# Score slots and down-projection parts as four 32x32 matmuls instead of one 32x128

## The chip, the cores and the metric

The kernel runs on one core of a Trainium2 chip. The metric is the device time of one execution in microseconds (us), the median over several runs. The core has five engines that work side by side and meet only at semaphores: TensorE (matmuls; its weight loads have a row of their own in the profile, PEld), VectorE (DVE), ScalarE (ACT), GpSimd (POOL) and SyncE (SP), which starts transfers. Matmul results land in PSUM, which has eight banks of 128 partitions x 512 float32; all other tiles (names ending in `_sb`) are in SBUF, 128 partitions wide.

TensorE's array has 128 rows (the contracted dimension) and 128 columns (the result's partitions). A matmul with a `tile_position` uses a part of the array whose sizes are multiples of 32, and matmuls on separate parts can run at once. Three shapes occur in the kernel: full (128 rows x 128 columns), column tiles (128 x 32, four side by side) and row tiles (32 x 128, four one under another). The profile writes them 128*128, 128*32 and 32*128.

## The reference

The input `x` is 2048 x 512. With `xn` the layer norm of `x`, the output is `x + s * g`:

- `s` is attention with 32 heads of 16 dimensions for the queries and a single shared head for keys and values: `q = xn @ wq`, `k = xn @ wk`, `v = xn @ wv`, softmax of `q k^T / 4` over 2048 keys, times `v`, and then `@ wo`.
- `g = silu(silu(xn @ w1) @ w2)`, where `w1` is 512 x 1792 and `w2` 1792 x 512.

All inputs are bfloat16. Because the contraction of a score is only 16 long (one head), a full-height matmul would leave most of the array's rows unused.

## The kernel before

**Tiling of the attention.** Queries are cut into four chunks of 512 and heads into four octets, which gives 16 tiles of q (`mk_q`, 128 partitions = eight heads x 16 dimensions, 512 queries). Two heads share a strip of 32 partitions, so each tile is handled as two groups `g` (32 groups in all), and in a group strip `i` (0 to 3) belongs to one head. `kt_sb` holds the transposed keys, repeated in each strip for the even and, shifted by 16 partitions with zeros, for the odd heads. One *score slot* is one strip `i` and one block `kt` of 128 keys: a matmul with 32 contracted rows (`kt_sb` 32 x 128 as the weights, `qt_sb` 32 x 512 as the moving operand) that fills a whole PSUM bank, 128 keys x 512 queries. There are 32 x 4 x 16 = 2,048 slots. `s_mm` issues one.

**Phases.** `do_S` puts three or four slots, with different strips and different banks, into one *score phase*. They sit in separate row groups of the array and run at once. Only the last matmul of a phase increments TensorE's semaphore. Banks 0 to 6 are shared by slots and jobs; bank 7 takes the attention's output.

**What follows a slot.** Most slots go to ScalarE (`act_step`, L1717), which takes the exponential of one to three banks at a time and writes `pa_sb`. The others go to VectorE (`pass_d`, L1002), which forms an approximate exponential with integer arithmetic (`db_sb`); GpSimd adds three shifted versions to it (`split`, L1202, `ds_sb`). `do_pv` (L1282) then multiplies all of these with the values: four column tiles at once, each 128 keys x 32 columns, into bank 7. `make_norm` divides by the sums.

**Jobs.** The other products (queries, `h` = the up projection, `z` = the down projection, `w` = the output projection) are jobs made by `product`. A job holds one bank and has rounds; a round is four column tiles (`col4`, L511), one contracted block of 128. If a phase has only three slots, a job can put one strip of 32 contracted rows of its last block into the idle row group: that is `piece` (L618), a 32-row matmul that adds into the job's bank. Four pieces make up one round. 76 matmuls are of this kind.

**What sets the order.** `Planner` and the steps below it (`pe_step`, `act_step`, `generic_step`) simulate the engines with fixed durations and write the order of every engine out before the program is built: `MM` = 216 ns for a matmul of 512 columns however many run at once, `SWITCH` = 105 ns between two modes of the array (`S` row tiles, `C` column tiles, `F` full), `T_P` and so on for the others. `finalize` turns the dependencies into semaphore waits, and each engine runs its list in order. `do_S` places a phase as one operation of 216 ns (two slots on the same strip would count double).

Of the kernel before, what the change touches and what calls it, by code (L numbers as in the profile page):

```python
# [15 lines left out]
P = 128  # L16
DH = 16
NQ = 512
LN_EPS = 1e-5
T_ISSUE, T_SWDGE = 450.0, 1000.0  # L20
J_BASE, J_END, MIXJ = 0.1, 1.0, 2
# [274 lines left out]
def bass_recurrent_scan__grouped_kv_mqa__dense_activation_silu__prompt_kernel(  # L296
# [14 lines left out]
    F = B_w1.shape[1]  # L311
    NT, NC, NDC, NFT = S // P, S // NQ, D // P, F // P
    NH = D // DH
# [5 lines left out]
    QSCALE = float(DH) ** -0.5  # L319
    assert D == 512 and S % NQ == 0 and F % P == 0  # L320

# [3 lines left out]
    NQR, NON = 4, 2 * NOC  # L325

    with ExitStack() as es:
        def sb(name, shape, dt):
            return es.enter_context(nc.sbuf_tensor(name, shape, dt))
# [10 lines left out]
        kt_sb = sb("kt_sb", [P, 2, S], BF16)  # L340
        v_sb = sb("v_sb", [P, K + 1, NKT, 48], BF16)
        qt_sb = sb("qt_sb", [P, NQR, NQ], BF16)
        pa_sb = sb("pa_sb", [P, NPA * NQ], BF16)
        db_sb = sb("db_sb", [P, NDB, 4 * NQ], U16)
        ds_sb = sb("ds_sb", [P, NDS, 4 * NQ], U16)
        f_sb = sb("f_sb", [P, 2, NQ], FP32)
# [31 lines left out]
        def bank(b):  # L378
            return ps[:, b * 512:(b + 1) * 512]
# [87 lines left out]
        for n in first:  # L467
            b = a + n
            tiles = range(a, b)
            g = a // 4  # L470
            y, w, h = rstd_sb[:, a:b], var_sb[:, 0, a:b], var_sb[:, 1, a:b]

            def dv(fn, reads, writes, pre):
                return pl.add(Task(DV, 66.0, fn, reads, writes, g, [pre] if pre is not None else []))
            t = pl.add(Task(DV, 66.0, lambda v, a=a, b=b, w=w: v.tensor_scalar(
                w, mv_sb[:, a:b, 1], LN_EPS, None, op0=ALU.add), [("mv", i) for i in tiles], [("ve", a)], g,
                [aggr[i] for i in tiles]))
# [31 lines left out]
        def col4(h, b, lhs, rhs, start, stop, n=NQ):  # L509
            for j in range(4):  # L510
                last = h.matmul(bank(b)[32 * j:32 * (j + 1), 0:n], lhsT=lhs(j), rhs=rhs, start=start, stop=stop,  # L511
                                tile_position=(0, 32 * j), skip_group_check=True)
            return last
# [93 lines left out]
        def product(jb, lhs, rhs, needs):  # L607
            n = len(jb.rounds)

            def rnd(k):  # L610
                def mk(b):
                    last = jb.left == 1
                    return lambda pe: col4(pe, b, lambda j: lhs(k, slice(0, P), 32 * j, 32), rhs(k, slice(0, P)), k == 0, last)
                return mk

            def piece(k, i, last):
                rows, b = slice(32 * i, 32 * i + 32), jb.bank
                return (lambda pe: pe.matmul(bank(b), lhsT=lhs(k, rows, 0, P), rhs=rhs(k, rows), start=False, stop=last,  # L618
                                             tile_position=(32 * i, 0), skip_group_check=True), needs(k))
            jb.rounds = [(rnd(k), needs(k), MM) for k in range(n)]  # L620
            jb.piece = piece

# [240 lines left out]
            return k  # L863

        def s_mm(pe, b, g, i, kt):
            return pe.matmul(bank(b), lhsT=kt_sb[32 * i:32 * i + 32, g % 2, kt * P:(kt + 1) * P],  # L866
                             rhs=qt_sb[32 * i:32 * i + 32, (g // 2) % NQR, :],
                             start=True, stop=True, tile_position=(32 * i, 0))

        def v_lhs(j, g, kt):  # L870
            return v_sb[:, j, kt, DH:48] if g % 2 == 0 else v_sb[:, j, kt, 0:32]
# [134 lines left out]
        def do_S(t):  # L1006
# [87 lines left out]
            def emit(pe, mm=tuple(mm)):  # L1094
                h = None
                for (b, g, i, kt) in mm:
                    h = s_mm(pe, b, g, i, kt)
                if extra is not None:
                    h = extra(pe)
                return h  # L1100
# [22 lines left out]
            while late and len(seen) < 4 and len(dslots) < (2 if bl < two else 1) and want_d():  # L1123
                used = set(seen)
                d = pick_d(used, t)
                if d is None:
                    break
                b = late.pop(0)
                _, g, i, kt = d
                seen[i] = 1  # L1130
                t1 = max(op.t0 + 10.0, pl.ready(PE, s_reads(g, i, kt), [("ps", b)]))
                pool_free.remove(b)
                pl.place(PE, MM, lambda pe, b=b, g=g, i=i, kt=kt: s_mm(pe, b, g, i, kt), s_reads(g, i, kt), [("ps", b)], t0=t1)
                pl.set_mode("S")
                pass_d(b, *d)
                dslots.append(d)
                st["late"] = st.get("late", 0) + 1
# [682 lines left out]
```

## Time and profile before

| | |
|---|---|
| median of 3 runs | 669.84 us (669.71 to 669.84) |
| span of the profiled execution, first to last instruction | 667.9 us |
| its own time | not listed apart; the span lies 1.94 us below the median |
| mean granted TensorE clock | 1.000 |
| matmuls / weight loads | 8,972 / 8,973 |
| score slots (L866) | 2,048, mean record 384 ns |
| parts of the down projection (L618) | 76, mean record 384 ns |
| exponentials on ScalarE (L1717) | 670, 617.0 us of records |
| VectorE on slots (L1002) | 736, 475.4 us of records |
| GpSimd shifts (L1202) | 544, 554.0 us of records |

How to read it: a record of a matmul lasts from its start to the modelled arrival of its last result, so records of matmuls that stream one after another overlap, and busy time is the union of the records. A group is written `line engine operation out<-in`, then the tile of the array as rows*columns, the operand, the count, and after the bar the busy time and the mean ns of one. In a timeline a line is a start in us, a length in us (from the first start to the last end where a count stands behind), and the operation. In a list of waits a line is who waited, for whom, the total in us, how often, and the longest.

### The profile page before, as it was taken

Reading aid. Unit: us, or ns where it says so; the run is one execution under the profiler, and the core shown is the slowest. Engines: PE = TensorE matmul, PEld = TensorE weight load, DVE = VectorE, ACT = ScalarE, POOL = GpSimd, SP = SyncE. Lnnn points to the kernel's source line nnn. Section 1 sums busy time; section 2 is a strip of 40 time slices with the busy share of each in tenths; the row PEclk is TensorE's granted clock in tenths of the full one; section 3 lists DMA queues with packets and bytes.
Section 4 is the critical chain, followed back from the end, with each engine's and each line's share of the span. In section 5 each row is a group of like instructions: output and inputs, shape, how many; then the busy total and the mean of one; then the engine's idle time right before and its main releaser. Section 6 shows DMA issues by size and latency. Waiting matters only on the chain.

```text
span 667.9 us, 21230 instructions
## 1 busy us (share of the span) xinstructions
PE 657.8 (98%) x8972; PEld 190.3 (28%) x8973; DVE 613.6 (92%) x1093; ACT 652.8 (98%) x767; POOL 561.9 (84%) x560
## 2 busy tenths in 40 slices
PE   8999999999999999999999999999999999999997
PEld 4322222222222222222222222222222322222222
DVE  8989999999899999989999899999999999998995
ACT  6999999999999999999999999999999999999997
POOL 3059889999898889998989888999899989897972
PEclk9999999999999999999999999999999999999999
DMA  9500000000000000000000010000000000000000
GB/s 302 164 9 2 3 1 2 2 3 2 1 2 18 19 18 18 1 2 2 2 2 2 18 32 18 2 2 2 2 2 2 2 18 18 17 18 2 2 2 33
DMA packets 11501, 12.86 MB, mean 19 GB/s; under 512 B 1808, under 2 KB 10768, under 8 KB 11408
## 3 DMA queue, kind: packets, MB, share of 16 engines
q1 hardware_dynamic: 10928, 10.78, 5.0%
q8 instruction: 72, 1.18, 0.7%
q0 software_dynamic: 192, 0.46, 0.2%
q10 hardware_dynamic: 288, 0.26, 0.1%
q14 instruction: 21, 0.17, 0.1%
HBM read 8.95 MB, written 2.10 MB: 17 GB/s over the span
## 4 chain that ended last, share of the span: by engine, by line
PE 88%; ACT 6%; DVE 4%; issue 1%; DMA 0%; ACTq 0%; DVEq 0%
PE ps L1282 38%; PE ps L866 29%; PE ps L511 20%; ACT pa_sb L1717 6%; DVE db_sb L1002 1%; DVE stats_sb L458 1%; ACT t_sb L669 1%; DMA ds_sb<-in_A_x_dram 0%; DVE fin_sb L719 0%; PE ps L527 0%; DVE xnT_sb L538 0%; DVE xn_sb L487 0%; DVE ob_sb L731 0%; DVE mv_sb L462 0%; DVE on_sb L1316 0%
## 5 line engine op out<-in xcount | busy, mean ns | idle before, releaser
L1717 ACT ACTIVATE pa_sb<-ps 128x1024 bf16<-128x1024 f32 (+2 forms) x670 | 617.0, 1027 | 4.8 <-PE ps L866 3.5
L1202 POOL INT64_ADD ds_sb<-db_sb x544 | 554.0, 1040 | 64.2 <-DVE otr_sb L1342 31.7
L1002 DVE TENSOR_SCALAR db_sb<-ps 128x512 uint16<-128x512 f32 x736 | 475.4, 683 | 40.0 <-PE ps L866 28.6
L1282 PE MATMUL ps<-ds_sb,v_sb 128*32 128x512 bf16 x2208 | 268.7, 383 | 0.0
L866 PE MATMUL ps<-qt_sb,kt_sb 32*128 32x512 bf16 x2048 | 251.2, 384 | 3.9 <-ACT pa_sb L1717 0.9
L1282 PE MATMUL ps<-pa_sb,v_sb 128*32 128x512 bf16 x1316 | 240.9, 382 | 0.0
L1282 PE MATMUL ps<-db_sb,v_sb 128*32 128x512 bf16 x736 | 169.3, 383 | 0.0
L866 PEld LDWEIGHTS ps<-qt_sb,kt_sb 32*128 32x128 bf16 x2048 | 62.8, 91 | 276.7 <-ACT pa_sb L1717 151.2
L1282 PEld LDWEIGHTS ps<-ds_sb,v_sb 128*32 128x32 bf16 x2208 | 65.6, 95 | 62.3 <-issue 44.6
L511 PE MATMUL ps<-xnT_sb,w_sb 128*32 128x512 bf16 x896 | 71.7, 383 | 0.0
L1282 PEld LDWEIGHTS ps<-pa_sb,v_sb 128*32 128x32 bf16 x1316 | 58.8, 95 | 37.9 <-issue 24.7
L511 PE MATMUL ps<-w_sb,u_sb 128*32 128x512 bf16 x820 | 64.1, 383 | 0.0
L1282 PEld LDWEIGHTS ps<-db_sb,v_sb 128*32 128x32 bf16 x736 | 42.2, 95 | 20.2 <-issue 14.7
L669 ACT ACTIVATE t_sb<-ps 128x512 bf16<-128x512 f32 x72 | 44.9, 623 | 0.0
L671 DVE SCALAR_TENSOR_TENSOR u_sb<-t_sb,ps 128x512 bf16<-128x512 bf16 x56 | 38.2, 683 | 1.0
L618 PE MATMUL ps<-w_sb,u_sb 32*128 32x512 bf16 x76 | 29.2, 384 | 0.0
L511 PEld LDWEIGHTS ps<-xnT_sb,w_sb 128*32 128x32 bf16 x896 | 17.1, 94 | 26.1 <-issue 21.1
L1359 POOL DMA_DIRECT2D kt_sb<-kt_sb x4 | 2.3, 566 | 23.9 <-DVE var_sb L481 8.1
L1338 DVE STREAM_TRANSPOSE f_sb<-ps 128x512 f32<-128x512 f32 x31 | 21.9, 706 | 0.0
L511 PEld LDWEIGHTS ps<-w_sb,u_sb 128*32 128x32 bf16 x820 | 15.2, 95 | 22.5 <-issue 19.3
L511 PE MATMUL ps<-wo_sb,on_sb 128*32 128x512 bf16 x256 | 18.9, 383 | 0.0
L511 PE MATMUL ps<-xnT_sb,wq_sb 128*32 128x512 bf16 x240 | 18.7, 384 | 0.1
(74 smaller groups left out, 180.8 us busy)
## 6 DMA issues: line engine op xcount, KB each, us to landing
w_sb<-in_B_w_dram SPq DMA_DIRECT2D x2, 1792.0 KB, 13.4
xr_sb<-in_A_x_dram SPq DMA_DIRECT2D x16, 128.0 KB, 2.6
out_dram<-ob_sb SPq DMA_DIRECT2D x16, 128.0 KB, 1.7
ds_sb<-in_A_x_dram SPq DMA_DIRECT2D x3, 512.0 KB, 6.6
wq_sb<-in_A_wq_dram SPq DMA_DIRECT2D x1, 512.0 KB, 4.9
wo_sb<-in_A_wo_dram SPq DMA_DIRECT2D x1, 512.0 KB, 16.2
kt_sb<-kt_sb POOLq DMA_DIRECT2D x4, 112.0 KB, 3.7
ds_sb<-in_A_x_dram ACTq DMA_DIRECT2D x2, 128.0 KB, 2.9
```

The source lines that it names most:

```text
L458: ts_ = pl.add(Task(DV, 593.0, lambda v, t=t: v.bn_stats(stats_sb[:, t, :], x_tile(t)), [xkey(t)], [("st", t)], 1 + j, gate=(lambda j=j: S ...
L511: last = h.matmul(bank(b)[32 * j:32 * (j + 1), 0:n], lhsT=lhs(j), rhs=rhs, start=start, stop=stop, tile_position=(0, 32 * j), skip_group_c ...
L618: return (lambda pe: pe.matmul(bank(b), lhsT=lhs(k, rows, 0, P), rhs=rhs(k, rows), start=False, stop=last, tile_position=(32 * i, 0), skip ...
L669: t1 = Task(AC, 490.0, lambda a: a.activation(t_sb[:, k, :], src, ACT.Tanh, scale=scale), [held], [("t", k)], 0, [t0])
L671: t2 = Task(DV, T_P, lambda v: v.scalar_tensor_tensor(out=dst, in0=t_sb[:, k, :], scalar=1.0, in1=src, op0=ALU.add, op1=ALU.mult), [held, ...
L866: return pe.matmul(bank(b), lhsT=kt_sb[32 * i:32 * i + 32, g % 2, kt * P:(kt + 1) * P], rhs=qt_sb[32 * i:32 * i + 32, (g // 2) % NQR, :], ...
L1002: bt.P[i] = pl.add(Task(DV, T_P, lambda v: v.tensor_scalar(db_sb[:, bt.b, i * NQ:(i + 1) * NQ], bank(b), 128.0 * LOG2E, 128.0 * (SHIFT_BET ...
L1202: whole["po"].append(pl.add(Task(PO, T_P64, lambda g, cols=cols: g.int64_add(ds_sb[:, s, cols].bitcast(U64), db_sb[:, bt.b, cols].bitcast( ...
L1282: h = pe.matmul(bank(OB)[32 * i:32 * (i + 1), cols], lhsT=lhs, rhs=rhs, start=s0, stop=s1, tile_position=(0, 32 * i), skip_group_check=True)
L1338: t1 = pl.add(Task(DV, T_TR, lambda v: v.transpose(f_sb[:, k, :], bank(OB)), [("ps", OB)], [("F", k)], 1, [norm.get(("m", g - 2))]))
L1359: kt1[c] = pl.add(Task(PO, T_SWDGE, lambda e: e.dma_start(kt_sb[DH:P, 1, cols], kt_sb[0:P - DH, 0, cols]), [("kt0", k) for k in range(4 * ...
L1717: op = pl.place(AC, 0.8333 * NQ * n + T_AF, lambda a: a.activation(pa_sb[:, s * NQ:(s + n) * NQ].rearrange("p (b n) -> p b n", n=NQ), ps3[ ...
```

## The change

A constant `SW = 32` is added. `s_mm` and `piece` each issued one matmul of 32 rows x 128 columns. Now each issues four, for columns 0 to 31, 32 to 63, 64 to 95 and 96 to 127 of the weights, at tile positions `(32 * i, c)`, into the partitions `c` to `c + 31` of the same bank. Moving operand, bank, accumulation flags and results are the same. The last of the four is what is returned, and so it carries the increment if the slot is the last of its phase. Nothing in the planner is changed, so the order and the waits of all engines are the same list as before.

```diff
+SW = 32
...
             def piece(k, i, last):
                 rows, b = slice(32 * i, 32 * i + 32), jb.bank
-                return (lambda pe: pe.matmul(bank(b), lhsT=lhs(k, rows, 0, P), rhs=rhs(k, rows), start=False, stop=last,
-                                             tile_position=(32 * i, 0), skip_group_check=True), needs(k))
+                def emit(pe):
+                    for c in range(0, P, SW):
+                        h = pe.matmul(bank(b)[c:c + SW, :], lhsT=lhs(k, rows, c, SW), rhs=rhs(k, rows), start=False, stop=last,
+                                      tile_position=(32 * i, c), skip_group_check=True)
+                    return h
+                return emit, needs(k)
...
         def s_mm(pe, b, g, i, kt):
-            return pe.matmul(bank(b), lhsT=kt_sb[32 * i:32 * i + 32, g % 2, kt * P:(kt + 1) * P],
-                             rhs=qt_sb[32 * i:32 * i + 32, (g // 2) % NQR, :],
-                             start=True, stop=True, tile_position=(32 * i, 0))
+            for c in range(0, P, SW):
+                h = pe.matmul(bank(b)[c:c + SW, :], lhsT=kt_sb[32 * i:32 * i + 32, g % 2, kt * P + c:kt * P + c + SW],
+                              rhs=qt_sb[32 * i:32 * i + 32, (g // 2) % NQR, :],
+                              start=True, stop=True, tile_position=(32 * i, c), skip_group_check=True)
+            return h
```

## The prediction

> **What bounds the kernel now.** I read the page first (busy shares, chain, groups), then the busy time of the steady stretch, then the waits, then TensorE's timeline at full resolution.
>
> The page, busy shares and the chain that ended last:
> ```profile
> PE 657.8 (98%) x8972; PEld 190.3 (28%) x8973; DVE 613.6 (92%) x1093; ACT 652.8 (98%) x767; POOL 561.9 (84%) x560
> ...
> PE 88%; ACT 6%; DVE 4%; issue 1%; DMA 0%; ACTq 0%; DVEq 0%
> PE ps L1282 38%; PE ps L866 29%; PE ps L511 20%; ACT pa_sb L1717 6%; DVE db_sb L1002 1%; DVE stats_sb L458 1%; ACT t_sb L669 1%; DMA ds_sb<-in_A_x_dram 0%; DVE fin_sb L719 0%; PE ps L527 0%; DVE xnT_sb L538 0%; DVE xn_sb L487 0%; DVE ob_sb L731 0%; DVE mv_sb L462 0%; DVE on_sb L1316 0%
> ...
> L866 PE MATMUL ps<-qt_sb,kt_sb 32*128 32x512 bf16 x2048 | 251.2, 384 | 3.9 <-ACT pa_sb L1717 0.9
> ...
> L618 PE MATMUL ps<-w_sb,u_sb 32*128 32x512 bf16 x76 | 29.2, 384 | 0.0
> ```
> TensorE and ScalarE are both busy 98%, but the chain is 88% TensorE. The two changed operations are L866 (2,048 score slots) and L618 (76 parts): 2,124 matmuls out of 8,972, and L866 alone is 29% of the chain. By its names (`w_sb,u_sb`) L618 is the down projection alone.
>
> The waits of the weight loads, the only place where TensorE waits for another engine (time, times, longest):
> ```profile
> PEld ps L866 <- ACT pa_sb L1717: 151.2, 355, 0.7
> PEld ps L866 <- DVE db_sb L1002: 106.6, 240, 0.7
> ...
> PEld ps L866 <- DVE qt_sb L628: 5.4, 12, 0.5
> ...
> PEld ps L866 <- DVE fin_sb L719: 4.4, 10, 0.5
> ```
> This is 267.6 us in 617 waits and looks like semaphores, but is not. The timeline of three microseconds shows what it is:
> ```profile
> 299.88 0.39 PE L866 MATMUL ps<-qt_sb,kt_sb 32*128 32x512 bf16 x3
> 300.20 0.39 PE L1282 MATMUL ps<-ds_sb,v_sb 128*32 128x512 bf16 x2
> 300.21 0.39 PE L1282 MATMUL ps<-pa_sb,v_sb 128*32 128x512 bf16 x2
> 300.43 0.61 PE L511 MATMUL ps<-xnT_sb,wq_sb 128*32 128x512 bf16 x8
> 300.97 0.39 PE L866 MATMUL ps<-qt_sb,kt_sb 32*128 32x512 bf16 x3
> 301.29 0.62 PE L511 MATMUL ps<-xnT_sb,wq_sb 128*32 128x512 bf16 x8
> 301.84 0.39 PE L866 MATMUL ps<-qt_sb,kt_sb 32*128 32x512 bf16 x3
> 302.16 0.40 PE L1282 MATMUL ps<-ds_sb,v_sb 128*32 128x512 bf16 x4
> ```
> Rows of column tiles (128*32) follow each other every 0.216 us. Between a phase of row tiles (32*128) and a run of column tiles, in either direction, the next start comes some 0.31 us after the last: about 97 ns of emptying the array. In that case the weight loads sit idle for 0.42 us whatever the semaphores do. 617 x 0.42 = 259 us, so real waiting for ScalarE and VectorE is only 267.6 - 259 = 8.5 us, and by the start stamps it lies in 92 phases (92 ns each). TensorE sets the pace.
>
> **The stamps in ns.** The trace has every start in ns; the timeline rounds to 10. Counted over the whole trace there are 641 phases of row tiles, 440 with three matmuls and 201 with four (440 x 3 + 201 x 4 = 2,124). What I use:
> - spacing of a load-matmul pair inside a phase: 3.35 ns. The same for the four pairs that open a run of column tiles: 3.33 ns;
> - first load to first matmul: 4.5 ns in a row-tile phase, 1.5 ns in a column-tile run;
> - last matmul's start to the first matmul of the next mode: 314.5 ns from row to column tiles, 311.5 ns from column to row tiles, 317 ns from row tiles to full 128*128 matmuls, 309 ns from full ones to column tiles, all with 512 columns;
> - a column run of a single round, its weights not loaded ahead: 322 ns to the next mode (19.02 us; also a run of three at 44.91 us).
>
> **The change, part by part.** Instructions: 3 x 2,124 = 6,372 more matmuls and as many weight loads; matmuls go from 8,972 to 15,344. Order, waits and semaphores do not change: one increment on a phase's last matmul, as now; the planner's costs are untouched. So the sum is over phases: time from a phase's first load to the next mode's first matmul.
>
> Before, three slots: 4.5 + 2 x 3.35 + 314.5 = 325.7 ns; four: 4.5 + 3 x 3.35 + 314.5 = 329.1 ns.
>
> After, three slots are 12 pairs of 32 columns, loaded like column tiles: 1.5 + 11 x 3.35 + 322 = 360.4 ns; four are 16 pairs: 1.5 + 15 x 3.35 + 322 = 373.8 ns. The 512 columns still stream at once in all tiles.
>
> Difference: 34.7 ns x 440 + 44.7 ns x 201 = 15.3 + 9.0 = 24.3 us. The parts (L618) are slots in these phases and so are in it.
>
> Unknown prices, with ends:
> - *Spacing of 12 to 16 pairs.* No stretch has more than four tiles at once. Low end: all parts start together, which makes every phase 1.5 + 322 = 323.5 ns, 2.2 to 5.6 ns shorter than now, -2 us in all. High end: 25 ns a matmul, the start-to-start of the 16-column matmuls of the value projection (L583), 9 x 25 to 12 x 25 ns a phase, some 159 us. I take 3.35: both kinds of phase with separate tiles and 512 columns show it, while L583's matmuls all use the same array.
> - *End of the phase.* 322 (loads not ahead, 32 columns) or 314.5 (128 columns). At 314.5 the sum is 24.3 - 641 x 7.5 ns = 19.5 us. I take 322, since the parts are of 32 columns.
> - *The emptying itself.* Ends: gone, or as now. Row tiles to full matmuls changes only the row size, full to column tiles only the column size, and each keeps its 95 to 103 ns. I take it as it is, for the new switch (32*32 to 128*32) is of the first kind.
> - *Waits that soak it up.* Of the 8.5 us none or all may go. A stalled phase waits 92 ns and each phase brings 35 ns, 38%: I take 3.2 us off.
>
> Nothing else covers the 24.3 us: in the steady stretch TensorE is busy throughout.
> ```profile
> 40.00:655.00 615.00, 613.47 (x8319) 171.03 (x8315) 571.79 (x954) 611.07 (x699) 552.98 (x544) 1.00 0.03 7
> ```
> Columns are the stretch, then TensorE, loads, VectorE, ScalarE, GpSimd, clock and DMA. ScalarE's 611 holds overlap of successive records (1,024-element exponentials can start 904 to 921 ns apart and last 1,048); by those least intervals it has 17.8 us to spare. It and VectorE get more slack. A slot's result comes 27 to 40 ns later to them, which counts only in the few waits above. Instruction supply: a three-slot phase with two rounds has 24 + 16 instructions in 0.9 us, 22 ns each; the zero-filled rounds (256 columns) ran 24 rounds of eight in 109 ns, 13.7 ns each, so I cost it at nothing. If that cover is gone it costs some ns a pair.
>
> Sum: +24.3 - 3.2 = +21.1 us. The profiled span is 667.9; the median of the three runs, 669.84, is 1.94 above it, the launch around the span, which I keep. 667.9 + 21.1 = 689.0, plus 1.94: 690.9 us, +3.1%.
>
> Two rules of the Trainium skill bear here. "TensorEngine Tiling (Array Packing)", Gotcha 2: Feature Incompatibilities, says that column tiling excludes Fast Weight Load; the trace agrees as far as 322 against 314.5 ns go, and with the rule the sum is 24.3 us, without it 19.5. "TensorE: Matmul & The Clock Gate", The mechanism, says that weight loads overlap with running matmuls only where the row group differs; that is the last rival below.
>
> **Rivals.** (1) *The emptying goes or shrinks, as 32*32 and 128*32 tiles have the same width.* For it: every switch in the trace has a 128-wide side, so this one is not shown. Against: the switches above cost the same whichever size changes. 641 x 2 x 97 ns = 124 us would leave TensorE; ScalarE then bounds, and its 17.8 us are the most that goes: 652 us, with a fixed order 656. It decides from 21.1 us / 1,282 = 16 ns off each switch. Chance 0.08.
> (2) *Loads of one column strip for different row groups get in each other's way*, 25 ns apart as in L583, rather than 13.4 (4 x 3.35): the last load comes (n-1) x 25 + 10 ns after the first, 60 and 85 ns rather than 37 and 50; 440 x 23 + 201 x 35 = 17 us more, 708 us. Against: the present loads of 128 columns cover every strip and follow at 3.35 ns. Chance 0.09, with any shortfall of instructions in it.
> (3) *Hidden*, since ScalarE paces: within 0.2%. The 8.5 us of waits against 613 us busy speak against it. Chance 0.03.
> (4) *A load waits for the matmul before it in the same row group.* The four parts of a slot would stream one after another: 6,372 x 216 ns = 1,376 us more, 2,046 us. Against: four column tiles share all rows, and their loads start 3.3 ns apart under running matmuls, so by that rule the trace disagrees. Chance 0.02.
> The forecast has 0.78.
>
> **How the numbers follow.** The forecast's own ends: 19.5 - 8.5 = +11 (681) to 24.3 with nothing soaked up (694), somewhat more if the spacing is 4 to 5 ns (700). The range goes from 682 to rival (2)'s 708; outside lie rivals (1), (3), (4) and a little of the rest, under 0.2. About 0.2% is what a measurement of this kernel tells from no change. Faster: rival (1) and a rest, 0.09; same: rival (3), 0.03; slower 0.88.
>
> **What would show it.** Right: 15,344 matmuls; the L866 group's busy time grows by about 641 x 37 ns, from 251 to some 273 us; a three-slot phase starts its 12 matmuls within 37 ns, and the next mode follows 322 ns after the last; VectorE's and ScalarE's busy time stays and their shares fall by 3%. Wrong: the next mode less than 300 ns after a phase's last matmul (rival 1); starts in a phase spread over 60 ns or more, or in steps after every fourth (rival 2); 216 ns between parts of one slot (rival 4); TensorE idle grown while the phase did not (3).

## The result, and the profile after

The changed kernel takes 692.59 us (median of 3 runs, 692.33 to 693.86) against 669.84 us. The ratio is 1.0346, 95% interval 1.0327 to 1.0365: slower by 22.8 us. The profiled execution has a span of 690.5 us and a time of 692.33. The forecast was 690.9 us within 682 to 708.

The page of the changed kernel: busy shares, instruction queue, chain, and the groups of the slots, their weight loads and the parts (the line numbers have moved by up to 7; L872 was L866, L621 was L618, L1289 was L1282):
```profile
span 690.5 us, 33975 instructions
...
PE 678.0 (98%) x15345; PEld 210.0 (30%) x15345; DVE 623.3 (90%) x1093; ACT 665.2 (96%) x767; POOL 561.0 (81%) x560
...
q8 instruction: 122, 2.00, 1.2%
...
PE 90%; DVE 5%; ACT 3%; issue 1%; DMA 0%; ACTq 0%
...
L872 PE MATMUL ps<-qt_sb,kt_sb 32*32 32x512 bf16 x8192 | 272.1, 385 | 5.2 <-ACT pa_sb L1724 0.9
...
L872 PEld LDWEIGHTS ps<-qt_sb,kt_sb 32*32 32x32 bf16 x8192 | 81.8, 87 | 279.3 <-ACT pa_sb L1724 151.6
...
L621 PE MATMUL ps<-w_sb,u_sb 32*32 32x512 bf16 x304 | 30.0, 385 | 0.0
```
TensorE has 6,373 more matmul records (6,372 matmuls; the profile before lacks the record of one) and is busy 20 us longer; L872 alone grew from 251.2 to 272.1 us. ScalarE's and VectorE's shares fell by 2 points each, although their busy times grew, from 652.8 to 665.2 us and from 613.6 to 623.3 us. The chain is TensorE's at 90%.

TensorE's timeline in three phases:
```profile
310.39 0.42 PE L872 MATMUL ps<-qt_sb,kt_sb 32*32 32x512 bf16 x12
310.74 0.39 PE L1289 MATMUL ps<-ds_sb,v_sb 128*32 128x512 bf16 x2
310.75 0.39 PE L1289 MATMUL ps<-pa_sb,v_sb 128*32 128x512 bf16 x2
310.96 0.60 PE L512 MATMUL ps<-xnT_sb,wq_sb 128*32 128x512 bf16 x8
311.50 0.42 PE L872 MATMUL ps<-qt_sb,kt_sb 32*32 32x512 bf16 x12
311.85 0.61 PE L512 MATMUL ps<-xnT_sb,wq_sb 128*32 128x512 bf16 x8
312.39 0.42 PE L872 MATMUL ps<-qt_sb,kt_sb 32*32 32x512 bf16 x12
```
The twelve matmuls of a three-slot phase still run at once, but a phase's records now cover 0.42 us instead of 0.39, and the next mode starts 0.35 us after the phase's first matmul instead of 0.32. By the stamps in ns, over all 641 phases (medians):

| | before | after |
|---|---|---|
| first to last matmul, three slots (440 phases) | 7 ns | 37 ns |
| first to last matmul, four slots (201 phases) | 10 ns | 50 ns |
| last matmul of a phase to the column tiles | 314.5 ns | 314.5 ns |
| last column tile to the phase's first matmul | 312 ns | 309 ns |
| first matmul to the phase's signal, three slots | 415 ns | 490 ns |
| first matmul to the phase's signal, four slots | 424 ns | 524 ns |
| waiting at phase starts (last matmul to the phase's first load, beyond 308 ns), in all | 8.2 us | 10.3 us |

The span's growth of 22.6 us is then accounted for in three items. The phases: 440 x 30 + 201 x 40 ns = 21.2 us, less 641 x 3 ns = 1.9 us because the first matmul follows its load sooner: 19.3 us. The waits: 2.1 us. And a single pause in the first stage, 1.05 us beyond the usual spacing, which the forecast did not have:
```profile
14.55 0.28 PE L512 MATMUL ps<-zer_sb 128*32 128x256 bf16 x4
15.46 1.29 DVE L459 BATCH_NORM_STATS2 stats_sb<-ds_sb 128x6 f32<-128x512 bf16 x2
15.72 0.10 PEld L512 LDWEIGHTS ps<-zer_sb 128*32 128x32 bf16 x4 [1.27 <-issue]
15.72 0.29 PE L512 MATMUL ps<-zer_sb 128*32 128x256 bf16 x4 [0.89 <-issue]
```
These are filler rounds on zeros; from the start of the last before the gap to the first after it 1.16 us pass, with no semaphore to wait for ("issue"). The sum, 22.45 us, is within 0.2 us of the 22.6 us.

### The profile page after: what moved, and what is told of

Its sections match the earlier page's. It is cut to its first block, busy times and chain, and to the rows that moved or that the text cites. A ratio compares the mean times of both kernels' runs of the same rounds, so it can differ in the third digit from the quotient of the medians.

```text
span 690.5 us, 33975 instructions
## 1 busy us (share of the span) xinstructions
PE 678.0 (98%) x15345; PEld 210.0 (30%) x15345; DVE 623.3 (90%) x1093; ACT 665.2 (96%) x767; POOL 561.0 (81%) x560
## 4 chain that ended last, share of the span: by engine, by line
PE 90%; DVE 5%; ACT 3%; issue 1%; DMA 0%; ACTq 0%
PE ps L1289 36%; PE ps L872 33%; PE ps L512 20%; DVE db_sb L1009 3%; ACT pa_sb L1724 3%; DVE u_sb L676 0%; DMA ds_sb<-in_A_x_dram 0%; PE ps L554 0%; PE ps L528 0%; DVE fin_sb L724 0%; PE ps L621 0%; PE ps L650 0%; DVE on_sb L1323 0%; DVE stats_sb L459 0%; ACTq L328 0%
## 5 line engine op out<-in xcount | busy, mean ns | idle before, releaser
L1724 ACT ACTIVATE pa_sb<-ps 128x1024 bf16<-128x1024 f32 (+2 forms) x670 | 628.3, 1011 | 15.1 <-PE ps L872 9.0
L1009 DVE TENSOR_SCALAR db_sb<-ps 128x512 uint16<-128x512 f32 x736 | 482.6, 685 | 53.7 <-PE ps L872 36.7
L872 PE MATMUL ps<-qt_sb,kt_sb 32*32 32x512 bf16 x8192 | 272.1, 385 | 5.2 <-ACT pa_sb L1724 0.9
L1289 PE MATMUL ps<-ds_sb,v_sb 128*32 128x512 bf16 x2208 | 268.7, 383 | 0.0
L1289 PE MATMUL ps<-pa_sb,v_sb 128*32 128x512 bf16 x1316 | 240.7, 382 | 0.0
L1289 PE MATMUL ps<-db_sb,v_sb 128*32 128x512 bf16 x736 | 169.3, 383 | 0.0
L872 PEld LDWEIGHTS ps<-qt_sb,kt_sb 32*32 32x32 bf16 x8192 | 81.8, 87 | 279.3 <-ACT pa_sb L1724 151.6
L1289 PEld LDWEIGHTS ps<-ds_sb,v_sb 128*32 128x32 bf16 x2208 | 65.6, 95 | 62.4 <-issue 45.9
L1289 PEld LDWEIGHTS ps<-pa_sb,v_sb 128*32 128x32 bf16 x1316 | 58.8, 95 | 37.8 <-issue 26.3
L1289 PEld LDWEIGHTS ps<-db_sb,v_sb 128*32 128x32 bf16 x736 | 42.2, 95 | 20.3 <-issue 15.2
L621 PE MATMUL ps<-w_sb,u_sb 32*32 32x512 bf16 x304 | 30.0, 385 | 0.0
L512 PEld LDWEIGHTS ps<-xnT_sb,w_sb 128*32 128x32 bf16 x896 | 17.2, 94 | 25.8 <-issue 21.1
L512 PEld LDWEIGHTS ps<-w_sb,u_sb 128*32 128x32 bf16 x820 | 15.2, 95 | 22.6 <-issue 19.3
```

Source lines behind the costliest of these rows:

```text
L621: h = pe.matmul(bank(b)[c:c + SW, :], lhsT=lhs(k, rows, c, SW), rhs=rhs(k, rows), start=False, stop=last, tile_position=(32 * i, c), skip_ ...
L872: h = pe.matmul(bank(b)[c:c + SW, :], lhsT=kt_sb[32 * i:32 * i + 32, g % 2, kt * P + c:kt * P + c + SW], rhs=qt_sb[32 * i:32 * i + 32, (g ...
L1009: bt.P[i] = pl.add(Task(DV, T_P, lambda v: v.tensor_scalar(db_sb[:, bt.b, i * NQ:(i + 1) * NQ], bank(b), 128.0 * LOG2E, 128.0 * (SHIFT_BET ...
L1289: h = pe.matmul(bank(OB)[32 * i:32 * (i + 1), cols], lhsT=lhs, rhs=rhs, start=s0, stop=s1, tile_position=(0, 32 * i), skip_group_check=True)
L1724: op = pl.place(AC, 0.8333 * NQ * n + T_AF, lambda a: a.activation(pa_sb[:, s * NQ:(s + n) * NQ].rearrange("p (b n) -> p b n", n=NQ), ps3[ ...
```

## The experiments

The theory after the result: what a phase pays is the spread of the starts of its matmuls, 3.35 ns for each; the emptying between two tile shapes is as before; the signal comes later still, and the waits hang on it; the pause is a lack of instructions. Each run was made beside the kernel before, whose median was 669.69 to 669.79 us.

### Two matmuls of 32x64

```diff
-SW = 32
+SW = 64
```


> Two matmuls of 32x64 a slot instead of four of 32x32, so 6 or 8 a phase instead of 12 or 16. Theory (each further load-matmul pair costs 3.35 ns of TensorE at the phase's end and some 5 ns of its signal): 440 x 10 + 201 x 13.4 ns = 7.1 us of phase, less up to 1.9 if the first matmul follows its load sooner, plus under 1 us of waits: 676 to 678 us; the last matmul of a phase starts 17 or 24 ns after the first, the signal comes some 425 or 435 ns after the last matmul. Rival (narrow tiles as such cost, by a fixed amount a phase): near 692 us if any column split costs it, near 670 if only 32 columns do.

Measured: 683.60 us, ratio 1.0207 (1.0191 to 1.0222). Both ideas missed: it is 6 us above the theory and 8 or 14 us off either form of the rival. The spread is as the theory had it: 17 and 23 ns from first to last matmul. But the next mode comes 328 ns after the last matmul instead of 314.5, and the signal 438 and 447 ns after it, 12 to 13 ns over the 425 and 435 expected. The groups of weight loads give a hint (columns: busy us and mean ns of one behind the bar); first of the kernel before, then of this one:
```profile
L866 PEld LDWEIGHTS ps<-qt_sb,kt_sb 32*128 32x128 bf16 x2048 | 62.8, 91 | 276.7 <-ACT pa_sb L1717 151.2
```
```profile
L872 PEld LDWEIGHTS ps<-qt_sb,kt_sb 32*64 32x64 bf16 x4096 | 76.4, 101 | 276.9 <-ACT pa_sb L1724 149.5
```
A load of 64 columns takes 101 ns, of 128 columns 91, of 32 columns (above) 87. The later end of the phases makes 13.5 ns x 641 = 8.7 us, and the spread 440 x 10 + 201 x 13 ns = 7.0 us, less 1.9 us as after the change and less 0.3 us of waits (7.9 us against 8.2): 13.5 us, against a measured growth of 13.8. So the cost has two parts, the number of matmuls and a later end of the phase; with 32 columns the second is nil. That the second comes from the length of the phase's last load is argued and not shown: against 32 columns the load grows by as much as the phase's end (14 ns), but against 128 columns by 10 ns only, and no run changes the load alone.

That 128 columns load faster than 64 agrees with the Trainium skill, "TensorEngine Tiling (Array Packing)", Gotcha 2: Feature Incompatibilities, by which narrow tiles do without Fast Weight Load. "TensorE: Matmul & The Clock Gate", LDWEIGHTS (loading the stationary operand), has the time as columns / 1.2 ns, which by estimate is 27 ns for 32 columns more; here the loads of 64 columns are 14 ns longer than those of 32, so the measurement decides for half of it.

### The same matmuls strip by strip

```diff
...
-                for (b, g, i, kt) in mm:
-                    h = s_mm(pe, b, g, i, kt)
-                if extra is not None:
-                    h = extra(pe)
+                for c in range(0, P, SW):
+                    for (b, g, i, kt) in mm:
+                        h = s_mm(pe, b, g, i, kt, [c])
+                    if extra is not None:
+                        h = extra(pe, [c])
```
(Not shown: `s_mm` and `piece` take the list of column starts in place of their own range.)


> The same 12 or 16 matmuls of a phase, issued column strip by column strip (strip 0 of every slot, then strip 1) instead of slot by slot. Theory (only the count matters): 692.6 us within 1 us, spacing 3.35 ns. Rival (loads of one column strip for different row groups hinder each other): spacing over 3.35 ns, 5 us or more slower; rival (loads in one row group hinder each other, partly): faster by as much.

Measured: 692.64 us, ratio 1.0341 (1.0326 to 1.0357). Spread 37 and 50 ns, next mode 314.5 ns later, waits 10.3 us: the same in every number. Neither loads of one strip nor loads in one row group hinder each other at 3.35 ns apart. The forecast's rivals (2) and (4) fall.

### Slots split and parts whole; parts split and slots whole

The first undoes the `piece` half of the change:
```diff
-                def emit(pe):
-                    for c in range(0, P, SW):
-                        h = pe.matmul(bank(b)[c:c + SW, :], lhsT=lhs(k, rows, c, SW), rhs=rhs(k, rows), start=False, stop=last,
-                                      tile_position=(32 * i, c), skip_group_check=True)
-                    return h
-                return emit, needs(k)
+                return (lambda pe: pe.matmul(bank(b), lhsT=lhs(k, rows, 0, P), rhs=rhs(k, rows), start=False, stop=last,
+                                             tile_position=(32 * i, 0), skip_group_check=True), needs(k))
```
The second undoes the `s_mm` half:
```diff
-            for c in range(0, P, SW):
-                h = pe.matmul(bank(b)[c:c + SW, :], lhsT=kt_sb[32 * i:32 * i + 32, g % 2, kt * P + c:kt * P + c + SW],
-                              rhs=qt_sb[32 * i:32 * i + 32, (g // 2) % NQR, :],
-                              start=True, stop=True, tile_position=(32 * i, c), skip_group_check=True)
-            return h
+            return pe.matmul(bank(b), lhsT=kt_sb[32 * i:32 * i + 32, g % 2, kt * P:(kt + 1) * P],
+                             rhs=qt_sb[32 * i:32 * i + 32, (g // 2) % NQR, :],
+                             start=True, stop=True, tile_position=(32 * i, 0))
```

> Score slots split in four, parts of the down projection whole (32x128), so 76 phases change the column width from 32 to 128 within 32 rows before the part. Theory (any change of tile shape empties the array): the part starts some 314 ns after the last slot matmul; 76 x (314 - 4 x 3.35) ns = 22.9 us more: 715 us. Rival (tiles of equal rows need no emptying): 692.6 - 76 x 3 x 3.35 ns = 691.8 us.

> Parts of the down projection split in four, score slots whole (32x128). Theory (any change of tile shape empties the array): 76 x some 0.31 us = 24 us over the kernel before, 693 to 694 us. Rival (tiles of equal rows need no emptying, only the count matters): 669.8 + 76 x 3 x 3.35 ns = 670.6 us, no difference that can be measured.

Measured: 716.22 us, ratio 1.0691 (1.0673 to 1.0708), and 694.18 us, ratio 1.0365 (1.0349 to 1.0380). The theory's numbers were 715 and 693 to 694. TensorE's timeline, slots split and parts whole:
```profile
303.88 0.42 PE L868 MATMUL ps<-qt_sb,kt_sb 32*32 32x512 bf16 x12
304.24 0.39 PE L619 MATMUL ps<-w_sb,u_sb 32*128 32x512 bf16 x1
304.55 0.82 PE L512 MATMUL ps<-w_sb,u_sb 128*32 128x512 bf16 x10
```
and parts split, slots whole:
```profile
291.68 0.39 PE L871 MATMUL ps<-qt_sb,kt_sb 32*128 32x512 bf16 x3
292.00 0.40 PE L621 MATMUL ps<-w_sb,u_sb 32*32 32x512 bf16 x4
292.33 0.39 PE L1287 MATMUL ps<-pa_sb,v_sb 128*32 128x512 bf16 x1
```
The part uses a row group that no slot of its phase uses, and it reads and writes other memory; still it starts some 0.32 us after the slots, 314 to 318 ns after the last one by the stamps, in all 76 phases. Equal rows do not spare the emptying, nor (in the changed kernel, 32*32 to 128*32) do equal columns. Rival (1) falls. It also shows why the two halves of the change belong together: splitting only the 76 parts costs more than splitting everything.

### As many matmuls, but tiles of 32x128

Each slot and part is four matmuls of 128 moving columns, chunk by chunk across the slots, with the same weights loaded each time.
```diff
+NW = 128
...
-            return pe.matmul(bank(b), lhsT=kt_sb[32 * i:32 * i + 32, g % 2, kt * P:(kt + 1) * P],
-                             rhs=qt_sb[32 * i:32 * i + 32, (g // 2) % NQR, :],
-                             start=True, stop=True, tile_position=(32 * i, 0))
+            for c in cs:
+                h = pe.matmul(bank(b)[:, c:c + NW], lhsT=kt_sb[32 * i:32 * i + 32, g % 2, kt * P:(kt + 1) * P],
+                              rhs=qt_sb[32 * i:32 * i + 32, (g // 2) % NQR, c:c + NW],
+                              start=True, stop=True, tile_position=(32 * i, 0))
+            return h
...
```
(Not shown: `piece` likewise, and the loop over the chunks in `do_S`.)

> As many loads and matmuls as after the change, but in tiles of 32x128: each slot and part is four matmuls of 128 moving columns with the same weights, chunk by chunk across the slots. Theory (cost is the spread of starts and ends of matmuls that all stream 512 columns; here the starts spread under the stream): the last matmul starts 3 x 56 + 10 = 178 ns after the first and the next mode 151 ns later, 4 to 8 ns a phase more than before, 672 to 675 us; the signal some 250 ns after the last matmul. Rival (the number of instructions costs as such): 690 us or more.

Measured: 674.83 us, ratio 1.0074 (1.0060 to 1.0088), within the theory's 672 to 675. The last matmul starts 185 (188) ns after the first and the next mode 144 ns later: 329 (332) ns instead of 322 (325), 7 ns a phase. So 15,344 matmuls are not dear as such. What costs is that matmuls which all stream 512 columns start 3.35 ns apart and so end as late; here the starts lie under the streams of the chunks before. The signal comes 238 (243) ns after the last matmul, as expected (some 250): 12 or 16 matmuls do not delay it if only three or four run at once. This run has the pause of the first stage too (1.50 us at 14.62 us).

### The first 60 slots whole

```diff
+            s_count[0] += 1
+            w = P if s_count[0] <= WHOLE else SW
-            for c in range(0, P, SW):
+            for c in range(0, P, w):
...
```
(`WHOLE` is 60; the matmul takes `w` for `SW`.)

> The first 60 slots (20 phases, up to 38 us) whole, everything after them split in four. Theory (the 1.16 us pause of TensorE at 14.56 us is a lack of instructions, the kernel after reaching its 449th before the second refill): no pause between 14 and 16 us, 1.05 us and 20 x 0.03 us = 0.6 us less, 690.9 us. Rival (the pause comes from something else): it stays, 692.0 us. The two times are hard to tell apart; the trace decides.

Measured: 691.42 us, ratio 1.0323 (1.0309 to 1.0337). TensorE's timeline at the place of the pause, first of the kernel before, then of this run:
```profile
14.44 0.39 PE L511 MATMUL ps<-zer_sb 128*32 128x256 bf16 x8
14.76 0.39 PE L866 MATMUL ps<-qt_sb,kt_sb 32*128 32x512 bf16 x3
```
```profile
14.50 0.40 PE L1293 MATMUL ps<-pa_sb,v_sb 128*32 128x512 bf16 x4
14.73 0.39 PE L512 MATMUL ps<-zer_sb 128*32 128x256 bf16 x8
15.05 0.39 PE L876 MATMUL ps<-qt_sb,kt_sb 32*128 32x512 bf16 x3
```
The pause is gone. All six runs with a pause there (after the change, and five of the experiments) stop after exactly the 449th instruction of TensorE (446 loads and matmuls, two semaphore waits and a drain); the four without one have not got that far by 15.70 us (422 to 440; the kernel before 429). The same six, and no other, stop once more after exactly the 705th instruction, 256 further on, in the middle of a phase at 22.4 to 22.7 us and for 82 to 357 ns. The instruction queue, whose line after the change stands above, had this line before it (packets, MB, share):
```profile
q8 instruction: 72, 1.18, 0.7%
```
All its packets are of 16 KB (16,384 bytes). The 50 more for 12,744 more loads and matmuls make some 64 bytes an instruction, so a packet holds some 255, about the distance between the two stops. The first packet starts at 13.2 us before and 13.4 us after the change and takes 1.1 us. That fits instructions that arrive late at the start: reaching that count early is what the six runs share. The supply itself has no record that shows the wait. The gain, 0.9 us by span and 1.2 by median, is less than the 1.65 us expected; where the rest went was not followed up.

### Whole phases where the signal matters, and where not

The waits grew though TensorE became slower. For each phase that waits for VectorE, the trace was followed back to the signal that VectorE itself had been waiting for: in most cases that of a four-slot phase one or two phases earlier. Where it was one phase earlier the wait grew by 51 ns on average (19 phases), two phases earlier by 31 ns (38 phases with VectorE's one operation between). By the table above, a four-slot phase signals 100 ns later after its first matmul, while TensorE gets through it only 40 ns later, and through a three-slot phase 30 ns: 60 ns for one phase, 100 - 40 - 30 = 30 ns for two. Two runs put this to the test; `WHOLE` holds the 59 phases' places in TensorE's list.
```diff
+            w = P if len(pl.order[PE]) in WHOLE else SW
...
-                    h = s_mm(pe, b, g, i, kt)
+                    h = s_mm(pe, b, g, i, kt, w)
...
```


> As after the change, but 59 phases (57 of four slots, 2 of three) stay whole: those whose signal VectorE is waiting for when a phase one or two later waits for VectorE. Theory (waits grow since a phase's signal comes 100 ns later after its first matmul where TensorE itself is only 40 ns longer): the phases save 57 x 37 + 2 x 27 ns = 2.2 us and each of the waits behind them shrinks by up to 60 ns, some 3.3 us: 687.1 us, with 6 to 7.5 us of waits at phase starts instead of 10.3. Rival (the waits come from TensorE's own pace and do not hang on the signal): 2.2 us less, 690.4 us, waits near 10.

> As the run before it, but 59 other phases of the same sizes stay whole, none of which a waiting phase hangs on. Both theories: 2.2 us less than after the change, 690.4 us, waits at phase starts near 10 us. The two runs are compared with each other: the difference is what the late signal costs (3.3 us by the theory, none by the rival).

Measured: 686.94 us, ratio 1.0259 (1.0245 to 1.0273), against 690.38 us, ratio 1.0313 (1.0299 to 1.0327). The list of waits, first after the change:
```profile
PEld ps L872 <- ACT pa_sb L1724: 151.6, 357, 0.8
PEld ps L872 <- DVE db_sb L1009: 109.0, 240, 0.8
```
then with the sources whole:
```profile
PEld ps L873 <- ACT pa_sb L1727: 151.6, 357, 0.8
PEld ps L873 <- DVE db_sb L1010: 105.4, 240, 0.7
```
then with the others whole:
```profile
PEld ps L873 <- ACT pa_sb L1727: 151.6, 357, 0.8
PEld ps L873 <- DVE db_sb L1010: 109.0, 240, 0.8
```
(time in us, times, longest). As before, 0.42 us of each wait is the emptying, so what counts is the difference: 3.6 us in the waits for VectorE, none in those for ScalarE. By the stamps the waiting at phase starts is 6.8 us against 10.3 us: against the kernel after the change, the 61 waits behind the sources fall from 6.9 to 3.4 us, and the others stay at 3.4. The two kernels have the same number of matmuls and differ by 3.4 us, all of it in the waits that hang on the signal. The late signal is shown as their cause.

No run was faster than the kernel before.

## Why the prediction was right, and where not

- **What bounds.** Right: TensorE's chain went from 88% to 90%, and nothing hid the growth. Rival (3) falls.
- **Count, order and spacing.** Right: 12 matmuls in 37 ns (36.9 worked out), 16 in 50 (50.3); 15,345 matmuls; L872 at 272 us (273 worked out).
- **First load to first matmul.** Right: 3 ns sooner, seen as 309 instead of 312 ns.
- **End of the phase.** Wrong size. I took 322 ns, from single rounds of column tiles with 32 columns; it is 314.5. The row was the wrong neighbour, and a thin one: it rests on two places, with tiles of 128 rows, and at one of them (19.02 us) the next mode is full matmuls, which follow later after row tiles too (317 ns). The loads there last 92 to 93 ns, not 87, which fits the later end but is not shown to cause it. With tiles of 32 columns after the change the next mode comes 314.5 ns later, so the 7.5 ns are no price of 32 columns as such. The other end of the bound, 314.5, was the right one. 4.8 us too much.
- **The emptying.** Right: it stays, and the runs with mixed phases show it for two switches that the kernel before did not have. (Against the 216 ns between rounds its rows leave 93 to 101 ns for it, not 95 to 103; and the row from full to column tiles is a single place.)
- **Waits that soak it up.** Wrong in sign: 3.2 us off in the sum, 2.1 us on in fact. I had written that a slot's result comes 27 to 40 ns later and counts little. I had moved the result with the last matmul's start; the signal is later by a further 45 to 59 ns.
- **Busy times.** Wrong: VectorE's and ScalarE's were to stay, and rose by 9.7 and 12.4 us, since busy time is the union of records and these now overlap less. The records of `pa_sb` even became shorter (1,027 to 1,011 ns on average). Only the fall of the shares came, 2 points for 3%.
- **Instruction supply.** Costed at nothing from a stretch of zero-filled rounds; right for the steady part, but 1.05 us in the first stage. What I had looked at was a rate; what ran out, by the two stops 256 instructions apart, was the stock at the start, though no record shows the supply itself.
- **The sum.** 24.3 - 3.2 = 21.1 us worked out; 19.3 + 2.1 + 1.05 = 22.45 us found. The forecast, 1.7 us from the median, owes its closeness to luck: errors of both signs, 5 us too much in the phases, 6.4 us too little in the waits and the pause.

## What to carry to other kernels

Matmuls on separate tiles run at once, but here their starts and their completions were paid for one by one; split a matmul that already fills its row group only if that removes something dearer than some 3.4 ns of array time and 8 ns of signal for each piece. Before mixing tile shapes, count the changes of shape, not the matmuls: one change in the middle of a phase (314 ns) cost as much here as some ninety additional pieces (3.35 ns). When a stage gets slower, do not assume that its waits shrink: compare how much later it signals with how much later it comes back for the answer.

## What was not expected of the hardware

- **A phase's signal lags by the number of its matmuls that run at once.** From the last matmul's start to the signal it is 409 ns with 3 matmuls, 414 with 4, 454 with 12 and 473.5 with 16: 5.0 ns for each. With 12 or 16 matmuls of 128 moving columns, three or four at once, it is 238 or 243 ns. The Trainium skill, "TensorE: Matmul & The Clock Gate", The cost: per-tile semaphore tail, gives 4.7 ns a tile, beside a fixed part for the increment; the trace agrees. By that figure the signals would come 42 or 56 ns later after the last matmul (an estimate, for 9 or 12 tiles more), which is what the forecast's term for the waits left out.
- **A load of 64 columns is slower than one of 128:** 101 against 91 ns, with 87 ns for 32, and the next mode comes 13.5 ns later than with either (328 against 314.5 ns).
- **A pause of 1.1 to 1.5 us after TensorE's 449th instruction** in every kernel that gets there before 15.7 us, and in no other, and a second, shorter one in the same kernels after the 705th.
